# New front of a fused layernorm, GLU and attention kernel: narrow weight blocks in one queue, rows in the other, dummy matmuls on constants, a new order of the first tiles, one column block in the accumulators

## The chip, the cores and the metric

The kernel runs on one core of a Trainium2 chip. The metric is the device time of one execution in microseconds (us), before 1287.0 us (median of 3 runs, 1286.76 to 1287.05). A profile is one execution; its span, from the first to the last instruction, is about 1.8 us shorter than its time.

Words: PE is the tensor engine, DVE the vector engine, ACT the scalar engine, SPq and ACTq the instruction queues of the sync and the scalar engine, from which loads are issued. A "row block" n is 128 rows of x; "x block" Q is 512 rows. A "column block" fc is 128 columns of the gate and up weights (Wg, Wu). PEld is the load of a matmul's stationary operand.

## The reference, cut to what matters

```python
xn = layernorm(x)                                   # x: 2048 x 512
s  = attention(xn @ wq, k_cache, v_cache) @ wo      # 32 heads of 128, 2048 keys
g  = silu((relu(xn @ W_gate) * (xn @ W_up)) @ W_down)   # 512 -> 1792 -> 512
return x + s * g
```

The first thing the kernel does is the gate and up product of the first 512 rows. It needs x (row blocks 0 to 3) and W_gate and W_up (512 x 1792 each, 14 column blocks), so it starts while those arrive. All that the change touches lies there, in the first 32 us ("the front"); the attention after it is left as it was.

## The kernel before

Loads: the first number of a block list is the first column block; rows of a weight load are as long as its column block, 256 B a column block.

```python
FCS = [0, 3, 8, 14]           # column blocks 0-2, 3-7, 8-13
warm_w = sem_ln1.sig(dve.memset(warm[:], 0.0))
load_x0(sp, 0)                             # row block 0
load_x0(act, 1)
load_w(sp, Wg_sb, wg_src, sem_wg, 0)       # gate weights, columns 0-2
load_w(act, Wu_sb, wu_src, sem_wu, 0)      # up weights, columns 0-2
load_x0(sp, 2)
load_x0(act, 3)
load_w(sp, Wg_sb, wg_src, sem_wg, 1)
load_w(sp, Wu_sb, wu_src, sem_wu, 1)
load_xq(1)                                 # x block 1, 512 rows
load_w(sp, Wg_sb, wg_src, sem_wg, 2)
load_w(sp, Wu_sb, wu_src, sem_wu, 2)
# ... x blocks 2 and 3, Wd
```

The head: each row block is centred by DVE, transposed by PE through the accumulators (two PSUM banks), copied to SBUF by ACT, and multiplied with column blocks 0 to 2, one tile per row block and column block (four gate and four up matmuls). `head_transpose` returns what its ACT copy signals.

```python
_wait(pe, warm_w)
warm_mm(10)                                # dummy matmuls on zeros
def head_ln():
    ctok = {0: head_transpose(0, head_center(0))}
    warm_mm(2)
    for n in range(4):
        if n + 1 < 4:
            ntok = head_center(n + 1)
        _wait(pe, ctok[n])
        head_tile(n, 0)
        if n + 1 < 4:
            ctok[n + 1] = head_transpose(n + 1, ntok)
        for fc in range(1, 3):             # two tiles behind each transpose
            head_tile(n, fc)
```

Then come column blocks 3 to 13 for all 512 rows. Each takes one of three ring slots (a pair of PSUM banks); a slot is free when ACT has taken the relu of the gate and DVE has multiplied it with the up part. Between these products DVE also does the layernorm statistics of x blocks 1 to 3 (`ln_task`).

```python
s = ring_acquire()                         # waits for ACT and DVE of the block three before
# ... 4 gate matmuls, 4 up matmuls
rtok = sem_relu.sig(act.activation(gr_sb[gk][:], ps_r[:, gb, :], ACTF.Relu))
h_tok = sem_h.sig(dve.tensor_tensor(hT[par][:, fc, :], gr_sb[gk][:], ps_r[:, gb + 1, :], ALU.mult))
ring_tok[s] = [rtok, h_tok]
if Q == 0:
    ln_task(fc)      # DVE: statistics; after 4 of them ACT: square root, in order
```

The softmax here doesn't subtract the row's maximum and nothing guards it: scores larger than these inputs give would overflow.

Of the kernel before, what the change touches and what calls it, by code (L numbers as in the profile page):

```python
# [5 lines left out]
BF16 = mybir.dt.bfloat16  # L6
F32 = mybir.dt.float32
ALU = mybir.AluOpType
# [21 lines left out]
def _wait(eng, tok):  # L30
    if tok is None:
        return
    sem, val = tok
    if val <= 0:
        return
    eng.wait_ge(sem.h, val)
# [15 lines left out]
def bass_recurrent_scan__mha_block_cached__glu_gated_reglu__prompt_kernel(  # L52
# [18 lines left out]
    NQ = 512  # L71
# [33 lines left out]
    with ExitStack() as es:  # L105
        _cnt = [0]

        def S_(shape, dt, name):
            _cnt[0] += 1
            return es.enter_context(nc.sbuf_tensor(f"{name}_{_cnt[0]}", shape, dt))  # L110
# [4 lines left out]
        def newsem(unit=1):  # L115
            _cnt[0] += 1
            return _Sem(es.enter_context(nc.semaphore(f"sem{_cnt[0]}")), unit)
# [13 lines left out]
        Wq_sb = [S_([128, DC, Dh], BF16, "Wq_sb") for _ in range(2)]  # L131
        Wo_sb = [S_([128, G, D], BF16, "Wo_sb") for _ in range(2)]
        PT = [S_([128, 2, NQ], BF16, "PT") for _ in range(NPB)]
        warm = S_([128, D], BF16, "warm")
        es_b = ExitStack()

        def SB_(shape, dt, name):
# [19 lines left out]

        sem_x = [newsem(16) for _ in range(QB)]
        sem_x0 = [newsem(16) for _ in range(4)]
        sem_wg = [newsem(16) for _ in range(3)]  # L160
        sem_wu = [newsem(16) for _ in range(3)]
        sem_xq = [newsem(16) for _ in range(QB)]
        sem_wd = newsem(16)
        sem_kt = [newsem(16), newsem(16)]
# [37 lines left out]
        with nc.Block() as block:  # L202

            @block.tensor
            def _(_pe_eng):
# [10 lines left out]
                for b in range(2):  # L216
                    tok_pool = sem_pool.sig(pool.memset(V_sb[b][:, :, Dh:VW], 2.0))

                FCS = [0, min(3, FC), min(8, FC), FC]
                HFC = 3  # L220
                wg_src = B_W_gate.rearrange("(c p) f -> p c f", p=128)
                wu_src = B_W_up.rearrange("(c p) f -> p c f", p=128)
# [1 line left out]
                def load_w(eng, dst, src, sems, k):  # L224
                    a, b_ = FCS[k] * 128, FCS[k + 1] * 128
                    if b_ > a:
                        sems[k].sig(eng.dma_start(dst[:, :, a:b_], src[:, :, a:b_]))
# [1 line left out]
                x0_tok = {}  # L229
                x_tok = {}  # L230

                def load_x0(eng, n):
                    x0_tok[n] = sem_x0[n].sig(eng.dma_start(x_sb[:, n:n + 1, :], x_t[:, n:n + 1, :]))

                def load_xq(Q):
                    x_tok[Q] = sem_x[Q].sig(
                        sp.dma_start(x_sb[:, 4 * Q:4 * Q + 4, :], x_t[:, 4 * Q:4 * Q + 4, :]))

                warm_w = sem_ln1.sig(dve.memset(warm[:], 0.0))
                load_x0(sp, 0)  # L240
                load_x0(act, 1)
                load_w(sp, Wg_sb, wg_src, sem_wg, 0)
                load_w(act, Wu_sb, wu_src, sem_wu, 0)
                load_x0(sp, 2)
                load_x0(act, 3)
                load_w(sp, Wg_sb, wg_src, sem_wg, 1)
                load_w(sp, Wu_sb, wu_src, sem_wu, 1)
                if QB > 1:
                    load_xq(1)
                load_w(sp, Wg_sb, wg_src, sem_wg, 2)  # L250
                load_w(sp, Wu_sb, wu_src, sem_wu, 2)
                for Q in range(2, QB):
                    load_xq(Q)
                sem_wd.sig(sp.dma_start(Wd_sb[:], B_W_down.rearrange("(c p) d -> p c d", p=128)))
# [101 lines left out]
                def head_transpose(n, ntok):  # L356
                    tp_ps = acc_bf[n % 2]
                    _wait(pe, acc_free[n % 2])
                    if n == 0:
                        _wait(pe, tok_pool)  # L360
                    _wait(pe, ntok)
                    ins = None
                    for c in range(DC):
                        ins = pe.transpose(tp_ps[:, c * 128:(c + 1) * 128],  # L364
                                           xc_sb[:, n, c * 128:(c + 1) * 128], ident[:])
                    ptok = sem_tp.sig(ins)
                    src = tp_ps[:, 0:DC * 128].rearrange("p (c q) -> p c q", c=DC)
                    _wait(act, ptok)
                    acc_free[n % 2] = sem_xa.sig(act.copy(xcT[:, :, n * 128:(n + 1) * 128], src))  # L369
                    return acc_free[n % 2]  # L370

                def warm_mm(k):
                    for _i in range(k):
                        pe.matmul(ps_r[:, 2 * NSLOT - 1, 0:D], warm[:, 0:128], warm[:], start=True, stop=True)  # L374

                def head_ln():
                    ctok = {0: head_transpose(0, head_center(0))}
                    warm_mm(2)
                    for n in range(4):
                        if n + 1 < 4:  # L380
                            ntok = head_center(n + 1)
                        _wait(pe, ctok[n])
                        head_tile(n, 0)
                        if n + 1 < 4:
                            ctok[n + 1] = head_transpose(n + 1, ntok)
                        for fc in range(1, HFC):
                            head_tile(n, fc)

                half_slots = []

                def head_tile(n, fc):
                    hs = slice(n * 128, (n + 1) * 128)
                    fs = slice(fc * 128, (fc + 1) * 128)
                    if n == 0:
                        half_slots.append(ring_acquire())
                    s = half_slots[fc]
                    for i, (W, sems) in enumerate(((Wg_sb, sem_wg), (Wu_sb, sem_wu))):
                        if n == 0 and fc == 0:
                            pe.wait_ge(sems[0].h, 16)
                        ins = None  # L400
                        for c in range(DC):
                            ins = pe.matmul(ps_r[:, 2 * s + i, hs], W[:, c, fs], xcT[:, c, hs],  # L402
                                            start=(c == 0), stop=(c == DC - 1))
                        if n == 3:
                            half_tok[(fc, i)] = (sem_gate if i == 0 else sem_gu).sig(ins)
# [39 lines left out]
                sig_free = [None, None]  # L445
                hT_free = [None, None]

                def finish_gate_up(Q, fc, s, gtok, gu_tok):
                    par = Q % 2
                    gb = 2 * s  # L450
                    gk = fc % NSLOT
                    _wait(act, gtok)
                    _wait(act, gr_free[gk])
                    rtok = sem_relu.sig(act.activation(gr_sb[gk][:], ps_r[:, gb, :], ACTF.Relu))  # L454
                    _wait(dve, gu_tok)
                    _wait(dve, rtok)
                    if fc == 0:
                        _wait(dve, hT_free[par])
                    h_tok = sem_h.sig(
                        dve.tensor_tensor(hT[par][:, fc, :], gr_sb[gk][:], ps_r[:, gb + 1, :], ALU.mult)  # L460
                    )
                    gr_free[gk] = h_tok
                    ring_tok[s] = [rtok, h_tok]
                    if Q == 0:
                        ln_task(fc)
                    return h_tok

                def emit_gate_up(Q):
                    qs = slice(Q * NQ, (Q + 1) * NQ)
                    h_tok = None  # L470
                    for fc in range(FC):
                        fs = slice(fc * 128, (fc + 1) * 128)
                        if Q == 0 and fc < HFC:
                            s = half_slots[fc]
                            finish_gate_up(Q, fc, s, half_tok[(fc, 0)], half_tok[(fc, 1)])
                            continue
                        s = ring_acquire()
                        gb = 2 * s
                        if fc == 0:
                            _wait_all(pe, xt_ready[Q])  # L480
                        xT, xs = (xcT, slice(0, NQ)) if Q == 0 else (xnT, qs)
                        if Q == 0 and fc in FCS:
                            k = FCS.index(fc)
                            pe.wait_ge(sem_wg[k].h, 16)
                            pe.wait_ge(sem_wu[k].h, 16)
                        ins = None
                        for c in range(DC):
                            ins = pe.matmul(ps_r[:, gb, :], Wg_sb[:, c, fs], xT[:, c, xs],  # L488
                                            start=(c == 0), stop=(c == DC - 1))
                        gtok = sem_gate.sig(ins)  # L490
                        for c in range(DC):
                            ins = pe.matmul(ps_r[:, gb + 1, :], Wu_sb[:, c, fs], xT[:, c, xs],  # L492
                                            start=(c == 0), stop=(c == DC - 1))
                        gu_tok = sem_gu.sig(ins)
                        h_tok = finish_gate_up(Q, fc, s, gtok, gu_tok)
                    return h_tok
# [39 lines left out]
                    hT_free[par] = ytok  # L536

                assert DC == 4 and QB >= 2 and FC >= 4 * (QB - 1) + 2
                _wait(pe, warm_w)
                warm_mm(10)  # L540
                head_ln()
                for Q in range(QB):
                    hlast = emit_gate_up(Q)
# [352 lines left out]
```

## Time and profile before

| | before |
|---|---|
| time, median | 1287.0 us |
| span | 1284.6 us |
| PE busy (page, part 1) | 1278.8 us |
| first gate tile starts | 6.21 us |
| column block 3 starts | 12.83 us |

The page's first part and the first line of its chain. Columns of part 1: engine, busy us, share of the span, count of instructions.

```profile
span 1284.6 us, 26946 instructions
...
PE 1278.8 (100%) x12040; PEld 835.2 (65%) x12040; DVE 380.6 (30%) x685; ACT 1001.7 (78%) x1109; POOL 13.2 (1%) x25
...
PE 99%; DVE 1%; ACT 0%; issue 0%; DVEq 0%
```

PE bounds the kernel from the front to the end. So what the change can give is what PE waits for. This is the view of waits of PE in the first 60 us (engine, line, what it waited for: us in total, times, longest):

```profile
PE ps_r L374 <- DVE warm L239: 1.2, 1, 1.2
PE ps_r L488 <- ACT gr_sb L454: 0.4, 1, 0.4
PE ps_r L402 <- ACT xcT L369: 0.2, 1, 0.2
```

Three waits and no more; they stand in the timeline (start, duration, engine, line, operation, tiles; in brackets idle time before it and what ended it). L374 is a dummy matmul, L364 the transposes, L369 the ACT copy, L402 the head tiles, L488 the later gate blocks, L460 DVE's product.

```profile
1.19 4.12 PE L374 MATMUL ps_r<-warm 128*128 128x512 bf16 x10 [1.19 <-DVE warm L239]
...
5.15 0.39 PE L364 MATMUL ps_acc<-ident,xc_sb 128*128 128x128 bf16 x4
...
6.21 0.40 PE L402 MATMUL ps_r<-xcT,Wg_sb 128*128 128x128 bf16 x4 [0.25 <-ACT xcT L369]
...
6.67 0.39 PE L364 MATMUL ps_acc<-ident,xc_sb 128*128 128x128 bf16 x4
...
7.79 0.39 PE L402 MATMUL ps_r<-xcT,Wg_sb 128*128 128x128 bf16 x4
...
12.03 0.39 PE L402 MATMUL ps_r<-xcT,Wu_sb 128*128 128x128 bf16 x4
...
12.83 1.02 PE L488 MATMUL ps_r<-xcT,Wg_sb 128*128 128x512 bf16 x4 [0.42 <-ACT gr_sb L454]
```

A group of four 128-column matmuls has a duration of 0.39 us, but the next group starts 0.22 us after it: the rest overlaps the next group. For accounts of time the distance of starts counts. From the start of the last group, 12.03, the next could begin at 12.25 and began at 12.83. The view names ACT as what PE waited for; the slot is free only when DVE's product of block 0 has ended as well, and in the timeline that product runs from 12.04 to 12.73 us.

### The profile page before, as it was taken

What the parts mean: (1) busy time and instruction counts of PE and PEld (TensorE: products, weight loads), DVE (VectorE), ACT (ScalarE), POOL (GpSimd) and SP (SyncE); (2) the same over time, 40 slices, a digit from 0 to 9 for tenths busy, and PEclk for the clock granted to TensorE, in tenths of its full rate; (3) what the DMA queues carried; (4) which work ended last, traced back from release to release, by engine and by line L of the source; (5) the groups of instructions that cost most, each with busy time, mean ns of one, the idle gap of its engine ahead of it and who ended that gap; (6) DMA issues with size and microseconds to landing.
All of it is one profiled execution on the core that took longest, in us unless ns stands there. A gap on an engine that the chain in (4) does not pass through costs nothing.

```text
span 1284.6 us, 26946 instructions
## 1 busy us (share of the span) xinstructions
PE 1278.8 (100%) x12040; PEld 835.2 (65%) x12040; DVE 380.6 (30%) x685; ACT 1001.7 (78%) x1109; POOL 13.2 (1%) x25
## 2 busy tenths in 40 slices
PE   9999999999999999999999999999999999999998
PEld 5444476666666666666666666666666666666665
DVE  6433311112222222222222222222222222234455
ACT  3322399998888888888888888888888888888884
POOL 2100000000000000000000000000000000000000
PEclk9999999999999999999999999999999999999999
DMA  9600123232222332332321322323323312333202
GB/s 262 131 1 1 22 48 53 62 55 38 36 53 46 71 55 50 55 70 51 54 47 31 66 47 53 55 67 55 55 51 71 54 34 38 51 67 55 51 13 75
DMA packets 240977, 72.13 MB, mean 56 GB/s; under 512 B 227808, under 2 KB 240864, under 8 KB 240864
## 3 DMA queue, kind: packets, MB, share of 16 engines
q1 hardware_dynamic: 240048, 69.76, 28.5%
q8 instruction: 96, 1.57, 0.5%
q10 hardware_dynamic: 816, 0.66, 0.2%
q14 instruction: 17, 0.14, 0.0%
HBM read 32.77 MB, written 2.10 MB: 27 GB/s over the span
## 4 chain that ended last, share of the span: by engine, by line
PE 99%; DVE 1%; ACT 0%; issue 0%; DVEq 0%
PE ps_acc L742 36%; PE ps_r L645 34%; PE ps_r L578 9%; PE ps_r L599 8%; PE ps_acc L511 4%; PE ps_r L488 4%; PE ps_r L492 4%; PE ps_r L779 1%; DVE fin_tmp L787 0%; PE ps_r L402 0%; PE ps_r L374 0%; DVE x_sb L803 0%; ACT gr_sb L454 0%; PE ps_acc L364 0%; ACT xcT L369 0%
## 5 line engine op out<-in xcount | busy, mean ns | idle before, releaser
L655 ACT ACTIVATE PT<-ps_r 128x1024 bf16<-128x1024 f32 x1024 | 952.5, 1054 | 167.7 <-PE ps_r L645 167.7
L742 PEld LDWEIGHTS ps_acc<-V_sb,PT 128*128 128x128 bf16 x8192 | 620.9, 98 | 241.8 <-ACT PT L655 3.5
L742 PE MATMUL ps_acc<-V_sb,PT 128*128 128x129 bf16 x8192 | 776.9, 220 | 0.0
L645 PE MATMUL ps_r<-QT_sb,KT_sb 128*128 128x512 bf16 x2048 | 754.5, 379 | 0.0
L672 DVE RECIPROCAL rz_sb<-ps_acc 128x4 f32<-128x4 f32 x127 | 23.2, 183 | 729.8 <-PE ps_acc L742 729.8
L645 PEld LDWEIGHTS ps_r<-QT_sb,KT_sb 128*128 128x128 bf16 x2048 | 194.9, 98 | 1.1 <-DVE QT_sb L589 0.4
L578 PE MATMUL ps_r<-xnT,Wq_sb 128*128 128x512 bf16 x512 | 130.9, 379 | 0.0
L599 PE MATMUL ps_r<-Wo_sb,OT_store 128*128 128x512 bf16 x448 | 114.6, 379 | 0.0
L589 DVE CAST QT_sb<-ps_r 128x512 bf16<-128x512 f32 x128 | 88.5, 691 | 48.2 <-PE ps_r L578 48.2
L578 PEld LDWEIGHTS ps_r<-xnT,Wq_sb 128*128 128x128 bf16 x512 | 49.8, 97 | 60.7 <-ACT PT L655 27.1
L675 DVE TENSOR_TENSOR Onorm<-ps_acc,rz_sb 128x512 bf16<-128x512 f32 x127 | 87.8, 691 | 4.4
L599 PEld LDWEIGHTS ps_r<-Wo_sb,OT_store 128*128 128x128 bf16 x448 | 43.8, 98 | 52.9 <-ACT PT L655 0.2
L454 ACT ACTIVATE gr_sb<-ps_r 128x512 bf16<-128x512 f32 x56 | 32.9, 595 | 49.2 <-PE ps_r L488 48.7
L612 DVE TENSOR_TENSOR s_acc<-s_acc,ps_r 128x512 f32<-128x512 f32 x96 | 66.0, 687 | 17.4 <-PE ps_r L599 17.4
L460 DVE TENSOR_TENSOR hT<-gr_sb,ps_r 128x512 bf16<-128x512 bf16 x56 | 38.4, 685 | 46.9 <-PE ps_r L492 42.2
L511 PE MATMUL ps_acc<-Wd_sb,hT 128*128 128x512 bf16 x224 | 49.0, 379 | 0.0
L492 PE MATMUL ps_r<-xnT,Wu_sb 128*128 128x512 bf16 x168 | 43.1, 379 | 0.0
L488 PE MATMUL ps_r<-xnT,Wg_sb 128*128 128x512 bf16 x168 | 43.1, 379 | 0.0
L511 PEld LDWEIGHTS ps_acc<-Wd_sb,hT 128*128 128x128 bf16 x224 | 21.9, 98 | 26.5 <-DVE g_sb L528 0.3
L519 ACT ACTIVATE sig_sb<-ps_acc 128x512 f32<-128x512 f32 x12 | 7.2, 597 | 29.5 <-PE ps_acc L511 29.5
L492 PEld LDWEIGHTS ps_r<-xnT,Wu_sb 128*128 128x128 bf16 x168 | 16.4, 98 | 19.8
L488 PEld LDWEIGHTS ps_r<-xnT,Wg_sb 128*128 128x128 bf16 x168 | 16.4, 98 | 19.8
(50 smaller groups left out, 182.1 us busy)
## 6 DMA issues: line engine op xcount, KB each, us to landing
V_sb<-in_A_v_cache_dram SPq DMA_DIRECT2D x32, 512.0 KB, 4.6
Wq_sb<-in_A_wq_dram SPq DMA_DIRECT2D x32, 128.0 KB, 2.5
Wo_sb<-in_A_wo_dram SPq DMA_DIRECT2D x8, 512.0 KB, 4.9
OT_store<-Onorm SPq DMA_TRANSPOSE x127, 2.4
Wd_sb<-in_B_W_down_dram SPq DMA_DIRECT2D x1, 1792.0 KB, 14.6
x_sb<-in_A_x_dram SPq DMA_DIRECT2D x3, 512.0 KB, 12.1
out_dram<-x_sb SPq DMA_DIRECT2D x6, 256.0 KB, 2.2
Wg_sb<-in_B_W_gate_dram SPq DMA_DIRECT2D x1, 768.0 KB, 12.0
```

Of the source, the lines that this page charges most:

```text
L460: dve.tensor_tensor(hT[par][:, fc, :], gr_sb[gk][:], ps_r[:, gb + 1, :], ALU.mult)
L488: ins = pe.matmul(ps_r[:, gb, :], Wg_sb[:, c, fs], xT[:, c, xs], start=(c == 0), stop=(c == DC - 1))
L492: ins = pe.matmul(ps_r[:, gb + 1, :], Wu_sb[:, c, fs], xT[:, c, xs], start=(c == 0), stop=(c == DC - 1))
L511: ins = pe.matmul(ps_acc[:, jb, 0:D], hT[par][:, fc, j * 128:(j + 1) * 128], Wd_sb[:, fc, :], start=(fc == 0), stop=(fc == FC - 1))
L578: ins = pe.matmul(ps_r[:, bank, :], Wq_sb[b][:, c, :], xnT[:, c, qs], start=(c == 0), stop=(c == DC - 1))
L589: etok = sem_qpe.sig(dve.tensor_copy(QT_sb[b][:, qs], ps_r[:, bank, :]))
L599: ins = pe.matmul(ps_r[:, bank, 0:D], OT_store[g % 2][:, hh, n * 128:(n + 1) * 128], Wo_sb[g % 2][:, hh, :], start=(hh == 0), stop=(hh == ...
L612: dve.tensor_tensor(s_acc[:, n, :], s_acc[:, n, :], ps_r[:, bank, 0:D], ALU.add)
L645: ins = pe.matmul(ps_r[:, 2 * s + tt, :], KT_sb[h % 2][:, t * 128:(t + 1) * 128], QT_sb[h % 2][:, qs], start=True, stop=True)
L655: act.activation(PT[pb][:], ps_r[:, 2 * s:2 * s + 2, :], ACTF.Exp, scale=scale)
L675: dve.tensor_tensor(Onorm[ob][:], o_ap, rz_sb[:].to_broadcast([128, 4, Dh]), ALU.mult))
L742: ins = pe.matmul(o_ap, PT[pb][:, tt, j * 128:(j + 1) * 128], V_sb[vb][:, t, 0:VW], start=(t == 0 and j % 2 == 0), stop=(t == KT - 1 and j ...
```

## The change

Its intent: let the dummy matmuls start earlier, let the first tiles start on small pieces of weight, keep weights and rows from queueing behind each other, and spare block 3 its wait for a ring slot. The diff, cut to its core (`finish_gate_up` and `emit_gate_up` take the two PSUM banks as views; cuts are marked with `# ...`):

```diff
-                FCS = [0, min(3, FC), min(8, FC), FC]
+                FCS = [0, 1, 2, 4, 9, FC]
# ... five semaphores instead of three for each of Wg and Wu; head_tile waits for columns 0, 1 and 2 one by one
-                warm_w = sem_ln1.sig(dve.memset(warm[:], 0.0))
# ... the loads shown above
+                load_x0(sp, 0, 0, 64)          # row block 0 in halves of 64 rows
+                load_x0(act, 0, 64, 128)
+                for n in range(1, 4):
+                    load_x0(act, n)
+                for k in range(len(FCS) - 1):
+                    if k == 4:
+                        load_xq(1)
+                    load_w(sp, Wg_sb, wg_src, sem_wg, k)
+                    load_w(sp, Wu_sb, wu_src, sem_wu, k)
-                        pe.matmul(ps_r[:, 2 * NSLOT - 1, 0:D], warm[:, 0:128], warm[:], start=True, stop=True)
+                        pe.matmul(ps_r[:, 2 * NSLOT - 1, :], ones_w, ones_r, start=True, stop=True)
# ... the rest of the old head_ln, shown above, with its warm_mm(2)
-                        for fc in range(1, HFC):
-                            head_tile(n, fc)
+                    c0 = head_transpose(0, head_center(0))
+                    n1 = head_center(1)
+                    warm_mm(1)
+                    _wait(pe, c0)
+                    head_tile(0, 0)
+                    c1 = head_transpose(1, n1)
+                    n2 = head_center(2)
+                    head_tile(0, 1)
+                    _wait(pe, c1)
+                    head_tile(1, 0)
+                    head_tile(1, 1)
+                    head_tile(0, 2)
+                    c2 = head_transpose(2, n2)
+                    n3 = head_center(3)
+                    head_tile(1, 2)
+                    _wait(pe, c2)
+                    head_tile(2, 0)
+                    head_tile(2, 1)
+                    c3 = head_transpose(3, n3)
+                    head_tile(2, 2)
+                    _wait(pe, c3)
+                    for fc in range(HFC):
+                        head_tile(3, fc)
# ... in emit_gate_up
-                        s = ring_acquire()
-                        gb = 2 * s
+                        if Q == 0 and fc == HFC:
+                            s = None               # block 3: the two accumulator banks
+                            _wait_all(pe, acc_free)
+                        else:
+                            s = ring_acquire()
+                        g_ps, u_ps = gu_banks(s)
-                _wait(pe, warm_w)
-                warm_mm(10)
+                warm_mm(9)
```

Four parts, then: dummies, accumulators, order, loads.

More of the change, by code (lines that the diff above doesn't have):

```diff
@@ L133, in bass_recurrent_scan__mha_block_cached__glu_gated_reglu__prompt_kernel @@
         PT = [S_([128, 2, NQ], BF16, "PT") for _ in range(NPB)]
-        warm = S_([128, D], BF16, "warm")
         es_b = ExitStack()
@@ L159, in bass_recurrent_scan__mha_block_cached__glu_gated_reglu__prompt_kernel @@
         sem_x0 = [newsem(16) for _ in range(4)]
-        sem_wg = [newsem(16) for _ in range(3)]
-        sem_wu = [newsem(16) for _ in range(3)]
+        sem_wg = [newsem(16) for _ in range(5)]
+        sem_wu = [newsem(16) for _ in range(5)]
         sem_xq = [newsem(16) for _ in range(QB)]
@@ L230, in _, with load_x0 @@
                 x_tok = {}
-                def load_x0(eng, n):
-                    x0_tok[n] = sem_x0[n].sig(eng.dma_start(x_sb[:, n:n + 1, :], x_t[:, n:n + 1, :]))
+                def load_x0(eng, n, lo=0, hi=128):
+                    x0_tok[n] = sem_x0[n].sig(eng.dma_start(x_sb[lo:hi, n, :], x_t[lo:hi, n, :]))
                 def load_xq(Q):
@@ L237, in load_xq @@
                         sp.dma_start(x_sb[:, 4 * Q:4 * Q + 4, :], x_t[:, 4 * Q:4 * Q + 4, :]))
-                warm_w = sem_ln1.sig(dve.memset(warm[:], 0.0))
-                load_x0(sp, 0)
-                load_x0(act, 1)
-                load_w(sp, Wg_sb, wg_src, sem_wg, 0)
-                load_w(act, Wu_sb, wu_src, sem_wu, 0)
-                load_x0(sp, 2)
-                load_x0(act, 3)
-                load_w(sp, Wg_sb, wg_src, sem_wg, 1)
-                load_w(sp, Wu_sb, wu_src, sem_wu, 1)
-                if QB > 1:
-                    load_xq(1)
-                load_w(sp, Wg_sb, wg_src, sem_wg, 2)
-                load_w(sp, Wu_sb, wu_src, sem_wu, 2)
+                load_x0(sp, 0, 0, 64)
[7 more added lines that the diff above has]
+                    load_w(sp, Wu_sb, wu_src, sem_wu, k)
                 for Q in range(2, QB):
@@ L370, in head_transpose @@
                     return acc_free[n % 2]
+                ones_w = nc.const_aps.tensor(1.0, [128, 128], BF16)
+                ones_r = nc.const_aps.tensor(1.0, [128, NQ], BF16)
                 def warm_mm(k):
                     for _i in range(k):
-                        pe.matmul(ps_r[:, 2 * NSLOT - 1, 0:D], warm[:, 0:128], warm[:], start=True, stop=True)
+                        pe.matmul(ps_r[:, 2 * NSLOT - 1, :], ones_w, ones_r, start=True, stop=True)
                 def head_ln():
-                    ctok = {0: head_transpose(0, head_center(0))}
-                    warm_mm(2)
-                    for n in range(4):
-                        if n + 1 < 4:
-                            ntok = head_center(n + 1)
-                        _wait(pe, ctok[n])
-                        head_tile(n, 0)
-                        if n + 1 < 4:
-                            ctok[n + 1] = head_transpose(n + 1, ntok)
-                        for fc in range(1, HFC):
-                            head_tile(n, fc)
+                    c0 = head_transpose(0, head_center(0))
[21 more added lines that the diff above has]
+                        head_tile(3, fc)
                 half_slots = []
@@ L397, in head_tile @@
                     for i, (W, sems) in enumerate(((Wg_sb, sem_wg), (Wu_sb, sem_wu))):
-                        if n == 0 and fc == 0:
-                            pe.wait_ge(sems[0].h, 16)
+                        if n == 0 and fc in FCS:
+                            pe.wait_ge(sems[FCS.index(fc)].h, 16)
                         ins = None
@@ L446, in _, with gu_banks @@
                 hT_free = [None, None]
+                def gu_banks(s):
+                    if s is None:
+                        return ps_acc[:, 0, :], ps_acc[:, 1, :]
+                    return ps_r[:, 2 * s, :], ps_r[:, 2 * s + 1, :]
                 def finish_gate_up(Q, fc, s, gtok, gu_tok):
                     par = Q % 2
-                    gb = 2 * s
+                    g_ps, u_ps = gu_banks(s)
                     gk = fc % NSLOT
@@ L453, in finish_gate_up @@
                     _wait(act, gr_free[gk])
-                    rtok = sem_relu.sig(act.activation(gr_sb[gk][:], ps_r[:, gb, :], ACTF.Relu))
+                    rtok = sem_relu.sig(act.activation(gr_sb[gk][:], g_ps, ACTF.Relu))
                     _wait(dve, gu_tok)
@@ L459, in finish_gate_up @@
                     h_tok = sem_h.sig(
-                        dve.tensor_tensor(hT[par][:, fc, :], gr_sb[gk][:], ps_r[:, gb + 1, :], ALU.mult)
+                        dve.tensor_tensor(hT[par][:, fc, :], gr_sb[gk][:], u_ps, ALU.mult)
                     )
                     gr_free[gk] = h_tok
-                    ring_tok[s] = [rtok, h_tok]
+                    if s is None:
+                        y_bank_free[:] = [h_tok, h_tok]
+                    else:
+                        ring_tok[s] = [rtok, h_tok]
                     if Q == 0:
@@ L476, in emit_gate_up @@
                             continue
-                        s = ring_acquire()
-                        gb = 2 * s
+                        if Q == 0 and fc == HFC:
+                            s = None
+                            _wait_all(pe, acc_free)
+                        else:
+                            s = ring_acquire()
+                        g_ps, u_ps = gu_banks(s)
                         if fc == 0:
@@ L487, in emit_gate_up @@
                         for c in range(DC):
-                            ins = pe.matmul(ps_r[:, gb, :], Wg_sb[:, c, fs], xT[:, c, xs],
+                            ins = pe.matmul(g_ps, Wg_sb[:, c, fs], xT[:, c, xs],
                                             start=(c == 0), stop=(c == DC - 1))
@@ L491, in emit_gate_up @@
                         for c in range(DC):
-                            ins = pe.matmul(ps_r[:, gb + 1, :], Wu_sb[:, c, fs], xT[:, c, xs],
+                            ins = pe.matmul(u_ps, Wu_sb[:, c, fs], xT[:, c, xs],
                                             start=(c == 0), stop=(c == DC - 1))
```

## The prediction

> **What bounds it now.** TensorE. The page gives PE 1278.8 us busy of a 1284.6 us span; the chain that ended last is 99% PE. The view of PE waits in the first 60 us lists only 1.2 us before the first dummy matmul, 0.4 us before column block 3 and 0.2 us before the first gate tile. So the front can give at most some 6 us (the first real gate tile starts at 6.21 us), and after block 3 PE has no wait. 2% (26 us) is out of reach.
>
> **Dummy matmuls.** They start at 1.19 us, released by DVE's memset of the dummy tile. Reading constants written at 0.31 us, they can start near 0.87. Ten dummies hold PE until the transposes at 5.15 us, although the centred rows are ready at 4.77. Nine from 0.87, each 0.427 us (the clock record goes to full at 4.85 us), end near 4.7. First gate tile: 5.85 instead of 6.21, a gain of 0.36 us. The Trainium skill ("TensorE: Matmul & The Clock Gate", Part 1) says the activity window is free-running, so the release may move by some tenths; the trace shows one release, 3.66 us after the first matmul.
>
> **Rows in halves.** Row block 0 may land 0.4 us earlier (now used at 3.47). The skill ("DMA: Bandwidth & Descriptors", Rules for kernel authors) says not to bother with partition halves, and the dummies end later than the rows: no gain expected.
>
> **Order of the head.** Before, two tiles (0.89 us) follow each transpose group (0.22) ahead of the wait for its copy. Transpose start to next usable tile is 1.04 us (6.67 to 7.71), so it was hidden. The new order leaves one tile (0.445 us) there, in three places: 1.04 - 0.22 - 0.445 = about 0.37 us of PE idle each, 1.1 us in all.
>
> **Block 3 in the accumulators.** Removes the 0.42 us gap before 12.83 us (PE waits for ring slot 0, freed by DVE's product ending at 12.73).
>
> Laid out in time, block 3 starts at 12.94 instead of 12.83: +0.1 (-0.36 + 1.1 - 0.42, less 0.2 of pipeline drain).
>
> **Weights.** Blocks of 1, 1, 2 columns mean rows of 256, 256 and 512 B instead of 768. The packet records show 18 ns for 256 B, 36 for 768, 46 for 1024, 57 for 1280. That is about 0.7 us more DMA time ahead of x block 2. The first blocks land in time (estimates: Wg0/Wu0 4.6/5.1, Wg1/Wu1 5.7/6.3, Wg2/Wu2 7.5/8.4 us); the up part of block 2 is needed near 8.3: a stall of 0 to 0.4 us. x block 2 now lands at 19.46 and DVE already waits 0.54 us for it; the product of block 5 ends at 21.04 and PE needs that ring slot at 21.46: 0.4 us of slack. Landing at 20.2 would eat it and delay PE some 0.2 us.
>
> **Total.** +0.1 (head), +0.1 (up block 2), +0.2 (x block 2), less some chance that I over-cost the gaps: 1287.2 us against 1287.0, range 1286.4 to 1288.0. Chances: faster by 2% 0.01, within 2% 0.98, slower 0.01.
>
> **Right if the profile shows:** dummies starting near 0.87; first gate tile near 5.85; PE waiting three times about 0.37 us on the ACT copy of the transposes; no gap before block 3, which starts at 12.9 +- 0.4; DVE waiting more than 0.54 us for x block 2; perhaps a PE wait near block 8 on ring slot 1; all after 45 us only shifted.
>
> **Wrong if:** the clock is released later or earlier than 4.85 us; weights land later than estimated (slow DMA engine, then over 1 us lost) ; copies return faster than 1.04 us, so the gaps vanish (a gain of 0.8 us); x block 2 lands earlier.

## The result, and the profile after

Median 1287.55 us (six runs: 1288.97, and five from 1287.42 to 1287.64) against 1286.9 us (six runs) of the kernel before: 0.65 us slower, within 2%. The ratio is 1.0007, 95% interval 0.9994 to 1.002. Such a ratio comes with each result and is not quite the ratio of the medians that are quoted. The intervals here are some 0.13% wide on either side, 1.7 us; where a smaller difference is read below, it rests on ranges of runs that do not overlap or on the account of time in the profiles, and this is said.

The profiled run is the slow one of the six, 1288.97 us. Its page and its view of waits:

```profile
span 1287.2 us, 26718 instructions
...
PE 1267.0 (98%) x11811; PEld 834.8 (65%) x12038; DVE 380.7 (30%) x684; ACT 1001.6 (78%) x1109; POOL 13.3 (1%) x25
```

```profile
PE ps_r L510 <- DVE hT L475: 1.3, 1, 1.3
PE ps_r L412 <- ACT xcT L364: 0.9, 3, 0.5
PE ps_r L372 <- PEq L902: 0.8, 1, 0.8
PE ps_acc L359 <- DVE xc_sb L349: 0.6, 1, 0.6
PE ps_r L412 <- DMA Wg_sb<-in_B_W_gate_dram: 0.4, 1, 0.4
```

PE's busy time seems to fall by 12 us. That is not work saved: 11811 matmuls are recorded beside 12038 weight loads, so some 230 matmul records are missing, and the weight loads' busy time is unchanged. The waits tell more: new ones on DVE, on the copies and on weights. The timeline (L372 dummies, L359 transposes, L412 head tiles, L510 later gate blocks, L475 DVE's product, L314 DVE's statistics):

```profile
0.78 3.39 PE L372 MATMUL ps_r<-const-bfloat16-1.0 128*128 128x512 bf16 x9 [0.78 <-PEq L902]
...
4.73 0.38 PE L359 MATMUL ps_acc<-ident,xc_sb 128*128 128x128 bf16 x4 [0.56 <-DVE xc_sb L349]
...
5.79 0.40 PE L412 MATMUL ps_r<-xcT,Wg_sb 128*128 128x128 bf16 x4 [0.46 <-ACT xcT L364]
...
6.25 0.39 PE L359 MATMUL ps_acc<-ident,xc_sb 128*128 128x128 bf16 x4
...
7.08 0.40 PE L412 MATMUL ps_r<-xcT,Wg_sb 128*128 128x128 bf16 x4 [0.44 <-DMA Wg_sb<-in_B_W_gate_dram]
...
7.59 0.40 PE L412 MATMUL ps_r<-xcT,Wu_sb 128*128 128x128 bf16 x4
...
8.71 0.39 PE L412 MATMUL ps_r<-xcT,Wg_sb 128*128 128x128 bf16 x4
...
9.24 0.40 PE L412 MATMUL ps_r<-xcT,Wu_sb 128*128 128x128 bf16 x4
...
10.54 0.40 PE L412 MATMUL ps_r<-xcT,Wg_sb 128*128 128x128 bf16 x4 [0.23 <-ACT xcT L364]
...
12.51 0.40 PE L412 MATMUL ps_r<-xcT,Wg_sb 128*128 128x128 bf16 x4 [0.23 <-ACT xcT L364]
...
13.64 0.39 PE L412 MATMUL ps_r<-xcT,Wu_sb 128*128 128x128 bf16 x4
...
14.07 0.81 PE L510 MATMUL ps_acc<-xcT,Wg_sb 128*128 128x512 bf16 x3
```

The landings of the weights, as the traces have them (the moment at which the semaphore of a load is complete, us):

| weights of | before: gate, up | the change: gate, up |
|---|---|---|
| column 0 | 5.55, 6.24 | 4.53, 5.41 |
| column 1 | 5.55, 6.24 | 7.03, 7.54 |
| column 2 | 5.55, 6.24 | 8.43, 9.20 |

So column 0 does land earlier, by 0.8 to 1.0 us, but columns 1 and 2 land later than in the kernel before, where one load brings all three.

Block 3 shows three gate matmuls; the first of four is one of the missing records. The other blocks' matmuls start 0.216 us apart, so it began near 13.85, where the last head group (13.64 + 0.22) left PE free: the wait before block 3 is gone. The account against before, in distances of starts:

- first gate tile at 5.79 instead of 6.21: 0.42 us gained;
- weights of columns 1 and 2: gate of column 1 could start at 6.47 and started at 7.08, its up part 7.31 and 7.59, the up part of column 2 8.93 and 9.24: 1.20 us lost;
- copies of row blocks 2 and 3: 0.40 us each, 0.80 us lost;
- before block 3: 0.58 us gained.

Sum: 1.0 us later at block 3 (13.85 against 12.83). Then another 1.5 us is lost before block 7, which could start at 20.76 and starts at 22.27. Its cause is on DVE (L326 is the square root on ACT):

```profile
15.84 0.69 DVE L314 BATCH_NORM_STATS2 stats<-x_sb 128x6 f32<-128x512 bf16 x1 [1.51 <-DMA x_sb<-in_A_x_dram]
...
20.55 0.30 ACT L326 ACTIVATE sqv<-mv,eps_sb 128x4 f32<-128x4 f32 x1 [5.04 <-DVE mv L319]
...
21.44 0.69 DVE L475 TENSOR_TENSOR hT<-gr_sb,ps_r 128x512 bf16<-128x512 bf16 x1 [0.92 <-ACT gr_sb L469]
...
22.05 0.69 DVE L314 BATCH_NORM_STATS2 stats<-x_sb 128x6 f32<-128x512 bf16 x1
...
22.27 1.02 PE L510 MATMUL ps_r<-xcT,Wg_sb 128*128 128x512 bf16 x4 [1.34 <-DVE hT L475]
```

x block 1 now lies behind the first 5-column weights, and DVE waits for it until 15.84. Four statistics later ACT takes the square root of them at 20.55, after 5.04 us of idleness, and only then the relu of block 4, which stands behind it in ACT's instructions although PE began block 4's gate product at 15.59; DVE's product of block 4 follows at 21.44, and it frees the ring slot of block 7. In before the first of these statistics ran without a wait:

```profile
12.65 0.69 DVE L319 BATCH_NORM_STATS2 stats<-x_sb 128x6 f32<-128x512 bf16 x1
```

### The profile page after: what moved, and what is told of

Read it like the earlier page. It is cut to its first block, busy times and chain, and to the rows that moved or that the text cites. A ratio compares the mean times of both kernels' runs of the same rounds, so it can differ in the third digit from the quotient of the medians. Undisturbed runs are those within 1.5% of the kernel's fastest.

```text
span 1287.2 us, 26718 instructions
## 1 busy us (share of the span) xinstructions
PE 1267.0 (98%) x11811; PEld 834.8 (65%) x12038; DVE 380.7 (30%) x684; ACT 1001.6 (78%) x1109; POOL 13.3 (1%) x25
## 4 chain that ended last, share of the span: by engine, by line
PE 84%; ACT 12%; issue 1%; DVE 1%; DMA 1%; SPq 0%; DVEq 0%; ACTq 0%
PE ps_acc L763 32%; PE ps_r L666 25%; ACT PT L676 12%; PE ps_r L599 9%; PE ps_r L620 8%; PE ps_acc L533 4%; PE ps_r L510 3%; PE ps_r L514 3%; DMA x_sb<-in_A_x_dram 1%; PE ps_r L800 1%; DVE fin_tmp L808 0%; SPq L226 0%; DVE hT L475 0%; DVE stats L314 0%; DVE x_sb L824 0%
## 5 line engine op out<-in xcount | busy, mean ns | idle before, releaser
L666 PE MATMUL ps_r<-QT_sb,KT_sb 128*128 128x512 bf16 x1837 | 675.1, 379 | 0.3
L475 DVE TENSOR_TENSOR hT<-gr_sb,ps_r 128x512 bf16<-128x512 bf16 x55 | 37.7, 686 | 49.2 <-PE ps_r L514 41.2
L510 PE MATMUL ps_r<-xnT,Wg_sb 128*128 128x512 bf16 x165 | 42.6, 379 | 0.2
L510 PEld LDWEIGHTS ps_r<-xnT,Wg_sb 128*128 128x128 bf16 x168 | 16.4, 98 | 19.8
```

The costliest lines, as they stand in the source:

```text
L475: dve.tensor_tensor(hT[par][:, fc, :], gr_sb[gk][:], u_ps, ALU.mult)
L510: ins = pe.matmul(g_ps, Wg_sb[:, c, fs], xT[:, c, xs], start=(c == 0), stop=(c == DC - 1))
L666: ins = pe.matmul(ps_r[:, 2 * s + tt, :], KT_sb[h % 2][:, t * 128:(t + 1) * 128], QT_sb[h % 2][:, qs], start=True, stop=True)
```

## The experiments

A rule of account that held for every profile: span = start of block 3 + time lost before block 7 + 1271.8 us, within 0.2 us. So all differences lie in the front. The table gives, per profile, the clock's release (when the record of the granted clock goes to full), the first gate tile, block 3, the lost time before block 7, the span, and the median of the timed runs with its difference to the runs of the kernel before on the same chip. Starts of block 3 with a star are worked out from the second matmul's, minus 0.216.

| kernel | clock full | first tile | block 3 | lost before 7 | span | median | minus before |
|---|---|---|---|---|---|---|---|
| before | 4.85 | 6.21 | 12.83 | 0 | 1284.6 | 1286.9 | |
| before_again | 4.18 | 6.09 | 12.70 | 0 | 1284.5 | 1286.70 | -0.15 |
| the change | 3.42 | 5.79 | 13.85* | 1.5 | 1287.2 | 1287.55 | +0.65 |
| after_again | 6.12 | 5.87 | 13.76* | 0.8 | 1286.4 | 1287.93 | +1.49 |
| after_xq1_first | 4.48 | 5.88 | 13.90* | 0 | 1285.7 | 1287.78 | +1.34 |
| only_order | 6.25 | 6.74 | 14.57* | 0 | 1286.4 | 1288.17 | +1.73 |
| only_loads | 5.97 | 6.74 | 14.77* | 0 | 1286.6 | 1288.36 | +1.92 |
| only_dummies | 9.96 | 7.20 | 15.10* | 0 | 1286.9 | 1286.43 | -0.05 |
| only_acc | 5.69 | 6.62 | 12.66* | 0 | 1284.5 | 1286.15 | -0.33 |
| before_dummies_acc | 5.57 | 6.08 | 12.44* | 0 | 1284.2 | 1286.06 | -0.42 |
| best_xq2 | 6.30 | 6.04 | 12.52* | 0 | 1284.3 | 1286.27 | -0.21 |
| loads_wide | 4.20 | 6.16 | 14.05 | 0 | 1285.9 | 1287.68 | +0.83 |
| narrow_two_queues | 6.33 | 6.74 | 14.99 | 0 | 1286.8 | 1288.58 | +1.73 |
| after_old_order | 5.13 | 5.89 | 15.46 | 0 | 1287.2 | 1288.87 | +2.02 |

The profiled run can be an unusual one of its kernel: that of only_dummies took 1288.70 us, its four other runs 1286.22 to 1286.71. All results were correct. Medians are of five runs (six for before and for the change in the first call, four for only_acc and best_xq2).

### The changed kernel again

No edit.

> The changed kernel once more, unedited, for a second profile. In the first one (1288.97 us, the slowest of its six runs; the other five 1287.42 to 1287.64) PE lost 1.34 us before block 7, behind x block 1 that landed near 15.8 us. Theory A (that wait belongs to slow draws of the DMA landing only, and the ordinary loss of 0.6 us comes from the head): this profile, if its time is near 1287.5, shows x block 1 landing before 14.8 and no PE wait before block 7, but block 3 again starting 0.7 to 1.0 us later than before (12.83). Theory B (the wait is there in every run): x block 1 lands after 15.0 and PE waits over 0.5 us before block 7 also in a run near 1287.5.

Median 1287.93 us (1287.55 to 1288.18), before on this chip 1286.44 (1286.20 to 1286.96): ratio 1.001, 95% interval 0.9998 to 1.0023. The ranges of runs do not overlap, so the change is slower here by 1.5 us; in the first call it was 0.65 us. The profile is of the slowest run, 1288.18, and shows x block 1 at 15.07, with 0.8 us lost before block 7 and block 3 0.93 us late. That is between the two theories: the wait before block 7 is there again, but smaller. Taking the rule of account, the other five runs of the first call (spans 1285.6 to 1285.8) have room for block 3 one us late and nothing more. So the head's loss is there in each profile of the change, and the wait before block 7 comes on top in some runs.

### x block 1 ahead of the 5-column weights

```diff
-                    if k == 4:
+                    if k == 3:
                         load_xq(1)
```

> The changed kernel with x block 1 loaded ahead of the two 5-column weight blocks 4 to 8 instead of behind them. Theory A: within 0.2 us of the changed kernel's ordinary 1287.5, because x block 1 was not last there; slow draws like 1288.97 disappear. Theory B: 0.5 to 1.3 us faster. In both, the DVE wait for x block 1 (1.5 us in the first profile) is gone and x block 1 lands before 12.5 us; the weights of block 4 still land before 15.6, when PE wants them.

The DVE wait for x block 1 is gone, the loss before block 7 is 0, and the span is what block 3 alone explains. The median, 1287.78 (1287.50 to 1288.16), is 0.15 us below that of the unedited change on the same chip, and the ranges overlap. As theory A had it: the misplaced x block costs something in slow draws, but it is not what makes the change slower. That the slow draws disappear is not shown by five runs.

### Each part alone: the order

```diff
 # kernel before, with head_ln of the change (two dummies kept behind the first transposes)
```

> The kernel before with the new order of the head tiles alone. Theory O (the lost cover of the transposes' copies is the main cost): three PE waits of 0.23 us by the record (0.37 us of lost issue time) each, block 3 starts 0.9 to 1.1 us later than 12.83, time 1287.6 to 1288.0. Theory L (the loads are the main cost, the order harmless): block 3 within 0.3 us of 12.83, time within 0.3 us of before. x block 2 cannot make it worse, since PE comes later to block 8.

Median 1288.17 (1288.02 to 1288.17), +1.73 us, ratio 1.0013, interval 1.0000 to 1.0025. Larger than expected. The view of waits and the timeline show the three copies:

```profile
8.26 0.40 PE L414 MATMUL ps_r<-xcT,Wg_sb 128*128 128x128 bf16 x4 [0.23 <-ACT xcT L369]
...
10.68 0.40 PE L414 MATMUL ps_r<-xcT,Wg_sb 128*128 128x128 bf16 x4 [0.23 <-ACT xcT L369]
...
12.64 0.40 PE L414 MATMUL ps_r<-xcT,Wg_sb 128*128 128x128 bf16 x4 [0.23 <-ACT xcT L369]
```

Each loses 0.39 to 0.40 us (the group before them started at 7.64, 10.06, 12.03, so PE was free 0.22 us later): 1.2 us, and theory O holds. The other 0.53 us of this profile is not the order: the first tile starts at 6.74 instead of 6.21, because the clock went to full at 6.25 instead of 4.85 and the ten dummies and the transposes ran slowly to the end. 1.2 + 0.53 is the 1.74 us by which block 3 is late. All five runs lie within 0.15 us of each other; whether the clock was late in the four without a profile was not seen, so the median's +1.73 is not a measure of the order alone.

### Each part alone: the loads

```diff
 # kernel before, with FCS, semaphores and loads of the change; head tiles wait for the
 # weights of columns 0, 1 and 2 one by one
```

> The kernel before with the new loads alone (column blocks 1, 1, 2, 5, 5; all weights on one queue; rows on the other; x block 1 behind block 4 to 8), old head order. The old order wants the up weights of column 2 near 7.6 us; in the first profile of the change they landed near 9.2. Theory L: PE waits 1 to 2 us in the head for weights, block 3 starts 14.0 to 14.8, time 1288.0 to 1289.5. Theory O, if loads landed earlier when they are not disturbed: waits under 0.5 us in all, time within 0.5 us of before.

Median 1288.36 (1287.88 to 1289.19), +1.92 us. PE waits for both halves of column 2:

```profile
8.63 0.40 PE L399 MATMUL ps_r<-xcT,Wg_sb 128*128 128x128 bf16 x4 [0.57 <-DMA Wg_sb<-in_B_W_gate_dram]
...
9.45 0.40 PE L399 MATMUL ps_r<-xcT,Wu_sb 128*128 128x128 bf16 x4 [0.42 <-DMA Wu_sb<-in_B_W_up_dram]
```

Counted by starts, the gate group could begin at 7.89 (the group before it began at 7.66) and the up group at 8.86: 0.74 + 0.59 = 1.3 us lost. The late clock again gives 0.53. Theory L holds as well. So the order and the loads each cost more than a microsecond alone, and both together, with the other two parts, no more than 0.65 to 1.5 us: they do not add up, since PE waits for weights in the same stretch in which it would wait for copies.

### Dummies alone, accumulators alone, both

```diff
 # only_dummies: no memset, constants as operands, warm_mm(9) and warm_mm(1)
 # only_acc: gu_banks, and s = None for block 3
 # before_dummies_acc: both
```

> The kernel before with the dummy matmuls on constants alone (nine, not ten, and one, not two, behind the first transposes). If the dummies were what the first transposes waited for: dummies start near 0.8 us, first gate tile at 5.8 to 5.9 instead of 6.2 to 6.7 (later where the clock is released later), 0.3 to 0.6 us faster than before, unless the gain is given back at block 8, whose slack behind x block 2 was 0.4 us. Rival (the rows, not the dummies, set the start): first gate tile stays at 6.1 or later, time within 0.2 us of before.

> The kernel before with column block 3 in the accumulators alone. If the ring slot is what block 3 waits for: no PE wait before block 3, 0.3 to 0.5 us faster, less if block 8 then waits for x block 2 (0.4 us of slack). Rival (the gap only moves to the next ring slot, block 4): time within 0.2 us of before and a new PE wait before block 4.

> Both of these parts, without the new order and the new loads. If x block 2 (landing near 19.4 us whatever PE does) leaves only 0.4 us of slack: the parts do not add up, about 0.4 us faster than before and a PE wait of 0.3 to 0.5 us before block 8. Rival (it lands earlier or has more slack): 0.7 to 1.0 us faster and no such wait.

only_dummies: 1286.43 against 1286.48 (1286.20 to 1287.10), no gain, where 0.3 to 0.6 us was expected; its profile is useless for the ordinary case (Wg landed at 7.1 us there and held the first tile until 7.20, and the clock went to full only at 9.96). only_acc: 1286.15 (1286.02 to 1286.52), -0.33 us, as expected, and PE no longer waits before block 3 nor before block 4. Both: 1286.06 (1285.81 to 1286.29), -0.42 us, ratio 0.9997, interval 0.9984 to 1.0009. Both ranges overlap that of before, so these gains rest on the profiles (block 3 at 12.66 and 12.44 instead of 12.83 and 12.70) and not on the times; and the 0.09 us between the two kernels says nothing of the dummies. The parts do not add up to the 0.9 us that the idle times promised, but not for the expected reason: there is no wait before block 8. What shows is a wait for the up weights of the first tile:

```profile
6.08 0.39 PE L403 MATMUL ps_r<-xcT,Wg_sb 128*128 128x128 bf16 x4 [0.32 <-ACT xcT L367]
...
6.63 0.40 PE L403 MATMUL ps_r<-xcT,Wu_sb 128*128 128x128 bf16 x4 [0.16 <-DMA Wu_sb<-in_B_W_up_dram]
```

The up group could start at 6.31 and starts at 6.63. PE, started earlier, meets the weights, which land no earlier for it: at 6.58 here, and between 6.11 and 6.66 in the other profiles with the old loads. Whether this caps only_dummies too was not seen in an ordinary run of it.

### x block 2 ahead of the last weights

```diff
+                load_xq(2)
                 load_w(sp, Wg_sb, wg_src, sem_wg, 2)
                 load_w(sp, Wu_sb, wu_src, sem_wu, 2)
-                for Q in range(2, QB):
+                for Q in range(3, QB):
```

> The same two parts with x block 2 loaded ahead of the last weight blocks (8 to 13), which are not wanted before 20 us. x block 2 lands before 16 us, the last weights before 20. If x block 2 was the limit: 0.7 to 1.0 us faster than before, and faster than the two parts alone by 0.3 to 0.5. Rival: same as the two parts alone within 0.15 us.

On top of the two parts: 1286.27 (1285.78 to 1287.82), not better than 1286.06. x block 2 was no limit; this step of my prediction falls.

### Before against itself

No edit.

> The kernel before, unedited, timed against itself: a null test, and a second profile of it. Ratio 1.000 within 0.0003. Open is whether the first profile (clock to full at 4.85 us, first gate tile at 6.21, block 3 at 12.83, x block 2 at 19.46) is typical. Theory C (the clock's release moves from run to run and shifts the first gate tile of this kernel between 6.2 and 6.7): another release time, first gate tile later if the release is later than 5.4. x block 2: if 19.46 was a slow draw, DVE does not wait for it here.

1286.70 (1286.31 to 1287.42) against 1286.85 (1286.51 to 1287.12): the null test gives 0.9999, and 0.15 us is what a median of five can be off. The clock went to full at 4.18 and the first tile started at 6.09; in only_order, only_loads and narrow_two_queues, which share the dummies with it, release came at 5.97 to 6.33 and the first tile at 6.74. So in kernels with these ten dummies a late release goes with a first tile 0.65 us later. At the early end it is no longer the dummies that PE waits for: in before_again the view of waits shows 0.4 us for the gate weights ahead of the first tile. They landed at 5.96, a limit to any earlier start with these loads. DVE waited for x block 2 here too (until 19.24), without PE being held up.

### What in the loads: narrow rows or one queue

```diff
 # loads_wide: kernel before, queues of the change, column blocks 3, 5, 6 kept (x block 1 ahead of the last)
 # narrow_two_queues: kernel before, column blocks 1, 1, 2, 5, 5; gate weights and row blocks 0, 2 on SPq,
 # up weights of columns 0 to 3 and row blocks 1, 3 on ACTq
```

> The kernel before with the new queues (row block 0 in halves, all weights on one queue, rows on the other) but the old column blocks of 3, 5, 6. Theory N (the narrow rows of 256 and 512 B are what makes the new loads late): within 0.3 us of before, PE waits in the head under 0.3 us. Theory Q (one queue for all weights, behind about 0.55 us of issue each, is what makes them late): the up part of block 0 lands 0.5 to 1.5 us later than the 6.3 us of before, PE waits for it before the second half of the first tile, time 0.5 to 1.5 us longer.

> The kernel before with the new narrow column blocks (1, 1, 2, 5, 5) but the old split: gate weights and even row blocks on one queue, up weights of columns 0 to 3 and odd row blocks on the other. Theory N: PE waits 0.8 us or more in the head for weights of columns 1 and 2, time 1.0 to 2.0 us longer, as with the new loads alone (1.9). Theory Q: waits under 0.4 us, time within 0.5 us of before.

loads_wide: 1287.68 (1287.55 to 1287.78), +0.83 us. narrow_two_queues: 1288.58 (1287.92 to 1290.43), +1.73 us. Neither theory alone. The windows of 4 to 8 us show the rate (columns: window, length, then busy us of PE, PEld, DVE, ACT, POOL, granted clock, DMA share, GB/s), first of before, then of narrow_two_queues:

```profile
4.00:8.00 4.00, 3.75 (x42) 2.51 (x41) 3.16 (x10) 1.17 (x2) 0.00 (x0) 1.00 1.06 359
```

```profile
4.00:8.00 4.00, 3.95 (x30) 2.15 (x28) 2.60 (x8) 1.78 (x4) 0.00 (x0) 1.00 0.98 278
```

278 GB/s instead of 359, with the DMA engines about as busy (0.98 and 1.06 in the last column but one). The changed kernel and loads_wide, which has the old rows in the new queues:

```profile
4.00:8.00 4.00, 2.42 (x30) 1.61 (x30) 3.67 (x10) 1.87 (x4) 0.00 (x0) 1.00 1.10 286
```

```profile
4.00:8.00 4.00, 2.38 (x21) 1.24 (x19) 2.23 (x6) 1.28 (x3) 0.00 (x0) 1.00 1.08 357
```

only_loads has 287. So narrow rows lower the rate, with one queue or two. The landings agree: in narrow_two_queues columns 0 and 1 alone (512 KB) are complete at 7.00 us, later than columns 0 to 2 (768 KB) in before, at 6.24. Not tested is a share of the new blocks' sizes: column 2 now comes in one load with column 3, which PE wants only after the head. loads_wide keeps the rate and loses by arrival: the up weights of block 0 are issued at 1.99 instead of 1.18, behind a row half and the gate weights (each issue takes 0.5 to 0.6 us of the queue), and share the engines with three row blocks.

```profile
7.65 0.40 PE L399 MATMUL ps_r<-xcT,Wu_sb 128*128 128x128 bf16 x4 [1.11 <-DMA Wu_sb<-in_B_W_up_dram]
```

They land at 7.61 instead of 6.24: 1.37 us later, for an issue 0.81 us later. Issue order and sharing were not taken apart.

### The changed kernel with the old order

```diff
 # the change, with head_ln of before (one dummy behind the first transposes)
```

> The changed kernel with the old order of the head tiles (dummies, accumulators and loads as changed). If the new order only fills the time in which the late weights of column 2 are waited for anyway, it costs nothing there: PE waits over 1.0 us for column 2 here, block 3 starts 13.5 to 14.3 against 13.8, time within 0.3 us of the changed kernel (1287.9 on this chip). Rival (the three waits for copies cost 1.1 us there too): 0.6 to 1.1 us faster than the changed kernel.

Median 1288.87 (1287.90 to 1289.49), +2.02 us over before, where the change has +0.65 and +1.49. The ratio's interval, 1.0002 to 1.0027, overlaps that of the change, and the chips differ, so the 0.5 us between them is not sure; but the rival, an old order that is 0.6 us or more faster, is refuted: given the new loads, the new order costs nothing that these runs show. The profile adds something not expected. Windows between the records of the granted clock:

```profile
5.13:8.54 3.41, 2.09 (x22) 1.12 (x20) 2.84 (x7) 1.17 (x2) 0.00 (x0) 1.00 1.20 299
8.54:11.95 3.41, 2.87 (x26) 2.61 (x27) 0.67 (x3) 0.33 (x1) 0.00 (x0) 0.50 1.07 359
11.95:15.36 3.41, 3.41 (x64) 3.41 (x63) 0.11 (x1) 1.66 (x4) 0.00 (x0) 1.00 1.08 358
```

After a window in which PE, waiting for rows and weights, was busy for 2.09 us, its clock was halved for 3.41 us; groups then started 0.43 us apart instead of 0.22. That the waits caused it is likely but not shown, since after 1.83 busy us in loads_wide the clock stayed full. Two of the five runs are near 1287.9 and three between 1288.9 and 1289.5. That these three are the runs with a halved clock is not borne out: such a stretch lowers the mean granted clock of a run to 0.999, as in the profiled one, and the slowest run, 1289.49, has 1.000.

## Why the prediction was right or wrong

The time was right: 1287.2 predicted, range 1286.4 to 1288.0, measured 1287.55; slightly slower, far within 2%. In part this is luck: errors of opposite sign cancelled, two of the four conditions under "Wrong if" came true (another release of the clock; late weights, with over 1 us lost), and in the second call the loss was 1.49 us, more than the 1.0 us that the range allows above 1287.0. Point by point:

- **Ceiling.** Right: the rule of account shows that nothing after 32 us moved by more than 0.2 us in any of the fourteen profiles.
- **Dummies.** Predicted start 0.87 and first tile 5.85; measured 0.78, and 5.79 and 5.87 in two profiles. The Trainium skill ("TensorE: Matmul & The Clock Gate", Part 1) calls the activity window free-running; the traces agree, with releases from 3.42 to 9.96 us and 3.413 us between the records of after_old_order. The release moved by 2.7 us between two runs of the change (3.42 and 6.12), not by "some tenths". What I missed is that this cuts both ways: with the old dummies a late release cost up to 0.53 us, and the earlier dummies make the first tile less dependent on it (5.79 at a release of 3.42, 5.87 at 6.12).
- **Rows in halves.** DVE took row block 0 at 3.28 and 3.16 instead of 3.47 and 3.40, some 0.2 us earlier. The prediction called the dummies last; in the profile of the change, where the clock was early, the centred rows were (a wait of 0.56 us). The advice of the Trainium skill ("DMA: Bandwidth & Descriptors", Rules for kernel authors) not to bother with partition halves was not tested by itself.
- **Order of the head.** Right in mechanism and size: 0.40 us per copy instead of 0.37, and all three alone in only_order. In the change two remain, because the first was hidden by a wait for weights.
- **Block 3.** Right; the gain is 0.58 us, since the idle figure of 0.42 counts only from the modelled end of the group before.
- **Weights: the mis-sized term.** "The first blocks land in time (estimates: Wg0/Wu0 4.6/5.1, Wg1/Wu1 5.7/6.3, Wg2/Wu2 7.5/8.4 us)" and a stall of 0 to 0.4 us. The first pair landed nearly so (4.53 and 5.41), column 1 came 1.2 to 1.3 us later than estimated (7.03 and 7.54) and column 2 0.8 to 0.9 us later (8.43 and 9.20); PE lost 1.2 us. I had priced the narrow rows from their packets and charged the difference to x block 2, far down the queue, but not to columns 1 and 2 themselves: the rate in the head fell from 359 to 286 GB/s. A slow DMA engine, which the prediction names as the risk, was not looked for; how the 1.2 us divide between rate, issue order and sharing stays open.
- **x block 2: wrong.** It held PE up in no run. In the change it did land later (20.91 instead of 19.44), but DVE, held up by x block 1, came for it only at 22.05 and took it without a wait. x block 1, which the prediction does not mention, is the one that came late, by its new place behind the 5-column weights, and it costs 0.8 to 1.5 us in slow draws.

The predicted loss of 0.4 us thus had the right sign and a near size, with a weight stall three times as large as its upper figure partly offset by copies hidden behind it and by a step that did not occur.

The lowest median is that of the kernel before with the dummies on constants and block 3 in the accumulators: 1286.06 us against 1286.48 before and 1287.93 for the change on the same chip. Against the change the ranges of runs are apart; against before they overlap, and the profile alone speaks for it.

## What to carry to other kernels

Cutting the first loads finer lets work start only if the pieces really land earlier: add up issue time and row length for the first pieces, not only for the last, and check the landing of each against the moment at which it is wanted. When tiles are reordered, count what stands between a producer and its consumer; one tile of 0.45 us does not hide a copy that returns after 1.04 us. Gains of a front are to be read at the point where the bounding engine runs without waits again, here the start of block 3, since parts that each gain or lose a microsecond alone overlap.

## What the Trainium skill lacked or had wrong

- "TensorE: Matmul & The Clock Gate", Part 1 gives in its table a drop to half clock after an idle window, and further on tells of a kernel in which short idle gaps were enough; it gives no busy share. Here one dropped for 3.41 us after a window in which PE was busy for 2.09 of 3.41 us (after_old_order), while a window with 1.83 us busy (loads_wide, from its release at 4.20) was followed by full clock. So a window need not be idle throughout, and by the profile's busy time no threshold separates these two.
- "DMA: Bandwidth & Descriptors", Specifications puts the line rate at 512 B and more. Here the median packet of 512 B took 28 ns in the change (27 to 34 in the other profiles with such rows), 256 B 18, 768 B 36 (before) and 1024 B 48: in bytes per ns 18 (15 to 19), 14, 21 and 21. 512 B is better than 256 but still short of 768.
- The same page, "Issuing engines are not separate DMA queues", says that issuing from several engines saves only issue time, usually small. In a front it is not small: an issue held SPq 0.5 to 0.6 us. And moving the up weights from the second queue to third place in one queue, with all further rows in the other, had them issued 0.81 us later but landed 1.37 us later (loads_wide, 7.61 against 6.24), at the same rate (357 against 359 GB/s), so more than issue time changed; by what was not taken apart.
- No part of these pages that I used says how far landings of one load spread from run to run: x block 1 was taken by DVE, which waited for it, at 15.84 and at 15.07 us in two runs of the change.
